# A linear-attention and mixture kernel: factors of 18 columns, x and y worked on in PSUM, ACT copying the halves, gates made for both halves by the array, and another order of the steps

## The chip, the cores and the metric

The kernel runs on one core of one Trainium2 chip. The metric is the device time of one execution in microseconds (us); of several runs the median counts. Five engines work side by side, each through its own queue in order: TensorE (PE, with its weight loads as PEld), VectorE (DVE), ScalarE (ACT), GpSimd (POOL) and SyncE (SP), which issues all the transfers here. PE writes its results to PSUM, which this kernel divides into eight tiles of 128 partitions by 512 numbers. The other tiles lie in SBUF.

## The reference

Eight batches, eight heads, 576 positions, 64 numbers per head. First a linear attention with exponential features, then a mixture of four experts with causal attention over the joined heads, two experts per position:

```python
def phi(x):
    proj = np.einsum('bhsd,df->bhsf', x, w_phi)
    proj = proj - np.max(np.abs(proj), axis=-1, keepdims=True)
    return np.concatenate([np.exp(proj), np.exp(-proj)], axis=-1)
q_p, k_p = (phi(q), phi(k))
kv = np.einsum('bhsf,bhsd->bhfd', k_p, v)
z = np.sum(k_p, axis=2)
num = np.einsum('bhsf,bhfd->bhsd', q_p, kv)
den = np.einsum('bhsf,bhf->bhs', q_p, z)[..., None] + 1e-06
attn_out = num / den
...
logits = x @ w_gate
topk = np.argpartition(-logits, K, axis=-1)[..., :K]
sel = np.take_along_axis(logits, topk, axis=-1)
w = np.exp(sel - sel.max(-1, keepdims=True))
w /= w.sum(-1, keepdims=True) + 1e-09
for e in range(E):
    q, k, v = x @ wq[e], x @ wk[e], x @ wv[e]
    scores = np.where(causal, -1000000000.0, scale * (q @ k.transpose(0, 2, 1)))
    a = np.exp(scores - scores.max(-1, keepdims=True))
    a /= a.sum(-1, keepdims=True) + 1e-09
    out += gate[e] * (a @ v @ wo[e])   # w where e is one of the two, else 0
```

Two divisions matter for what follows. The first stage divides num by den, once for each position and head. The second multiplies a @ v by the gate over the sum of the row. In both the number to multiply by is the same for all 64 numbers of a head: a *factor* per position.

## The kernel before, in words

**The order.** The kernel is written as many small generators (streams). Each yields a `Step`: an engine, the keys that it needs, whether it takes a PSUM tile, and a condition. A planner (`Plan.loop`) holds all the streams, picks among those that could start soonest the one with the lowest position, and emits its instructions; `in_order` fixes that order on each engine. Positions come from the tables at the top (`POS1` for the first stage, `POS` for the second, `BOFF` per batch, `SLOPE`, `NPOS`, `HOT`). The planner keeps its own clocks with costs per instruction (`dve`, `act`, `copies`, `PORT` for a DVE instruction that meets POOL). None of that runs on the chip; it only sets which instruction stands behind which. Eight PSUM tiles "c" are shared by all the steps: a step of PE takes one, `plan.release` gives it back.

**First stage, per pair of heads (32 pairs).** `stream_k` projects the keys (L439, and L263 for the last 64 positions), `center` takes the largest absolute value (L486) and subtracts it (L500), ACT makes both exponentials, `key_sum` adds (L473). `stream_kv` multiplies by v (L527) and makes the sums z (L543); DVE transposes the result into `kvt` (L562), which goes through DRAM (`kvd`) and comes back as `kv`. `stream_q` projects the queries (L439), ACT copies them out as `u`, POOL reduces over the partitions (L602), DVE subtracts (L604), ACT makes both exponentials. `stream_n` makes the denominators (L629), spread over four groups of 32 partitions by halves and heads, and then the numerators (L640) for the two parts of the positions, 256 and 320 wide.

**Factors.** `fractions` turns denominators (called with 'd', 32 times) or sums of the attention (called with 'y' from `sums`, 16 times) into a tile of factors laid out as the numerators are. L650: DVE transposes 288 columns from PSUM into `wided` or `widey`, in blocks of 32; the PSUM tile is released at once. L653: the nine columns that differ are taken out, plus the small constant, into `few`. For 'd', L660 makes two reciprocals of 64 partitions and L662 two copies to the other half of the partitions. For 'y', L665 makes one reciprocal and L669 four multiplications by the gate `gc`, one for each pair of source and target halves. Then ACT or DVE spreads the 18 columns to 576 (L272 or L284, `wided<-bothd`), and L675 transposes them into `xf` or `rb`.

**x and y.** `divide` multiplies the numerators in PSUM by `xf` into `xf` itself (L681) and releases the PSUM tile; a copy rounds that to `xh`, and L267 subtracts (`sub_lo`) for the rest `xl`. `evac_y` does the same with `rb` (L954), `yh` and `yl`. The next pair's `xf` may be written when both parts of x are done.

**Second stage, per batch.** `proj_t` projects queries and keys of two experts at a time (L263, weights `qk`), `proj_v` values and gate logits (`vg`), `scores` makes the scores (L768), `mask` masks on POOL (L870), `maxima` takes the maxima on DVE (L883) and over the partitions on POOL (L887), DVE subtracts (L891), ACT makes the exponentials, `sums` sums them on PE (L914), `attend` multiplies by the values (L942), `project_out` makes the output (L263, `wo`). `gates` makes the gates on DVE (L820 to L838) and spreads them with small matmuls against the identity (L849) into 20 columns, which are copied to `gc`.

Of the kernel before, what the change touches and what calls it, by code (L numbers as in the profile page):

```python
# [63 lines left out]
PORT = 500.0  # L64
OTHER = 2.37
# [172 lines left out]
def tile_linear_attn_moe(ctx, tc, qt, kt, v, wts, out):  # L238
# [104 lines left out]
    spreads = {a: [(sb(f"wide{a}{i}", [128, S]), sb(f"few{a}{i}", [128, 9]), sb(f"both{a}{i}", [128, 9, 2])) for i in range(NX)] for a in "dy"}  # L343
# [267 lines left out]
    def stream_n():  # L611


        for p in range(NPAIRS):
# [8 lines left out]
            pk, ps = yield Step('PE', Pk + [kvk], 'c', ready, tiling=(128, 32)), rank(p) + NPOS[0]
            for c in range(2):
                for half in range(2):
                    for h in range(2):
# [2 lines left out]
                        nc.tensor.matmul(ps[g:g + 32, 0:S // 2].rearrange("p (a i) -> p a i", i=32), kvi[:, 2 * h + c, 64:96],  # L629
                                         P_[h][c].rearrange("p (a b i) -> p b a i", b=2, i=32)[:, half], start=c == 0, stop=c == 1, skip_group_check=True)  # L630
            plan.spawn(fractions('d', p, ps, pk, 1e-6, xf, ['xf'], has('x', p - 1) if p else None, ('rb', p)), rank(p) + POS1['evd'])
            for s0, s1 in PARTS:
                pk, ps = yield Step('PE', Pk + [kvk], 'c', has('rb', p), tiling=(128, 32)), rank(p) + NPOS[1]
                n = s1 - s0
                for c in range(2):
                    for h in range(2):
                        for k in range(2):
                            g = 64 * k + 32 * h
# [1 line left out]
                            nc.tensor.matmul(ps[g:g + 32, 0:n], kvi[:, 2 * k + h, 32 * c:32 * c + 32], P_[h][c][:, s0:s1], start=c == 0, stop=c == 1,  # L640
                                             skip_group_check=True)
                plan.spawn(divide(p, s0, s1, pk, ps), rank(p) + POS1['div'])
            done.add(('num', p))

    def fractions(a, n, ps, pk, eps, out, wk, free, flag, gate=None):
# [4 lines left out]
        dve(S // 2, [key], [pk], 1.13).transpose(X[:, 0:S // 2], ps[:, 0:S // 2])  # L650
# [2 lines left out]
        dve(9, [bk], [key]).tensor_scalar(out=C, in0=X[:, 0:S // 2:32], scalar1=eps, scalar2=None, op0=ALU.add)  # L653
        halves = [(0, 0), (1, 1), (0, 1), (1, 0)]
        if gate is None:
            for src, dst in halves:
                r, w = slice(64 * src, 64 * src + 64), slice(64 * dst, 64 * dst + 64)
                yield Step('DVE', [bk], hot=True)
                if src == dst:
                    dve(9, [bk], [], 6.0).reciprocal(both[w, :, src], C[r])  # L660
                else:
                    dve(9, [bk], []).tensor_copy(both[w, :, src], both[r, :, src])  # L662
        else:
            yield Step('DVE', [bk], hot=True)
            dve(9, [bk], [], 6.0).reciprocal(C, C)  # L665
            for src, dst in halves:
                r, w = slice(64 * src, 64 * src + 64), slice(64 * dst, 64 * dst + 64)
                yield Step('DVE', [bk, 'gc'], pred=has('gate', n // 2), hot=True)
                dve(9, [bk], ['gc']).tensor_tensor(out=both[w, :, src], in0=C[r], in1=gate[r], op=ALU.mult)  # L669
            done.add(('gated', n))  # L670
# [4 lines left out]
        dve(S, wk, [key], 1.13).transpose(out, X)  # L675
        done.update((('wide', a, n), flag))

    def divide(p, s0, s1, pk, ps):
# [2 lines left out]
        dve(n, [('x', s0)], [pk, 'xf']).tensor_tensor(out=xf[:, s0:s1], in0=ps[:, 0:n], in1=xf[:, s0:s1], op=ALU.mult)  # L681
# [1 line left out]
        st = Step(copies_sb(n), [('x', s0)], pred=has('px', (p - PXB) // NP) if p >= PXB else None, port=True)
        yield st
        copy(st.eng, n, xT[i][0][:, s0:s1], xf[:, s0:s1], [f'xh{i}'], [('x', s0)], 0.52)
        yield Step('DVE', [f'xh{i}'])
        sub_lo(n, xT[i][1][:, s0:s1], xf[:, s0:s1], xT[i][0][:, s0:s1], f'xl{i}', [('x', s0), f'xh{i}'])
# [128 lines left out]
    def gates(b):  # L816
# [26 lines left out]
        for g in range(2):
            for a in range(2):
                for half in range(2):
                    for e in range(2):
                        r, c = 64 * half + 32 * e, 64 * a + 32 * half
                        plan.run('PE', 16, [kc], [G], tiling=(128, 32))
                        nc.tensor.matmul(o[r:r + 32, g, :, a], ident[:, c:c + 32], gw[:, 5 * (2 * g + e):5 * (2 * g + e) + 5], start=True, stop=True, skip_group_check=True)  # L849
        st = Step(copies(20), [kc], pred=lambda: not b or (('gated', 2 * b - 1) in done and ('gated', 2 * b - 2) in done), hot=True)  # L850
# [22 lines left out]
    def maxima(n):  # L873
# [29 lines left out]
    def sums(n):  # L903
# [45 lines left out]
    def evac_y(b, g, s0, s1, pk, ps):  # L949
        hi, lo = (t[:, s0:s1] for t in ys[g])  # L950
        m, i = s1 - s0, (2 * b + g) % RB
        rb = yf = rbs[i][:, s0:s1]
# [3 lines left out]
        st = Step(copies_sb(m), [('yf', i, s0)], hot=True, port=True)
        yield st
        copy(st.eng, m, hi, yf, [('yh', g, s0)], [('yf', i, s0)], 0.52)
        yield Step('DVE', [('yh', g, s0)], hot=True)
        sub_lo(m, lo, yf, hi, ('yl', g, s0), [('yf', i, s0), ('yh', g, s0)])  # L960
# [99 lines left out]
```

## Time and profile before

| | us |
|---|---|
| median of 3 runs | 689.44 |
| lowest and highest | 684.30, 689.53 |
| the profiled execution | 685.02 |
| its span, first to last instruction | 683.2 |
| ACT busy within the span | 407.9 |
| POOL busy within the span | 248.9 |

The profile is of one execution. A group's busy time is the sum of its instructions' durations. Matmuls are pipelined and the ends of their records are modelled, so a busy PE is not PE at its densest. What ended the idle time of an engine is inferred from semaphores. `ps_c` stands for any of the eight PSUM tiles, and buffer numbers are left out of the names.

### The profile page before, as it was taken

What the parts mean: (1) busy time and instruction counts of PE and PEld (TensorE: products, weight loads), DVE (VectorE), ACT (ScalarE), POOL (GpSimd) and SP (SyncE); (2) the same over time, 40 slices, a digit from 0 to 9 for tenths busy, and PEclk for the clock granted to TensorE, in tenths of its full rate; (3) what the DMA queues carried; (4) which work ended last, traced back from release to release, by engine and by line L of the source; (5) the groups of instructions that cost most, each with busy time, mean ns of one, the idle gap of its engine ahead of it and who ended that gap; (6) DMA issues with size and microseconds to landing.
All of it is one profiled execution on the core that took longest, in us unless ns stands there. A gap on an engine that the chain in (4) does not pass through costs nothing. (4 is left out here: it accounts for less than half of the span.)

```text
span 683.2 us, 20283 instructions
## 1 busy us (share of the span) xinstructions
PE 638.9 (94%) x8364; PEld 484.4 (71%) x8364; DVE 629.7 (92%) x1385; ACT 407.9 (60%) x803; POOL 248.9 (36%) x167
## 2 busy tenths in 40 slices
PE   9999998969999999979989999899999898999997
PEld 7655777547976787647776676676768666788896
DVE  6899999979999999999979999999998999899884
ACT  4876666736764685465665656765477554465462
POOL 5425235722156205720446322442524532052330
PEclk9999999979999999999999999999999999999999
DMA  6643440212223221333303234203341030101002
GB/s 188 184 132 94 109 135 21 75 45 61 63 63 106 66 79 51 100 106 106 109 2 98 74 97 124 80 28 107 98 112 49 21 113 12 48 14 70 2 35 106
DMA packets 43691, 54.34 MB, mean 80 GB/s; under 512 B 20432, under 2 KB 26576, under 8 KB 43600
## 3 DMA queue, kind: packets, MB, share of 16 engines
q1 hardware_dynamic: 43600, 53.05, 26.6%
q8 instruction: 66, 1.08, 0.7%
q14 instruction: 25, 0.20, 0.1%
HBM read 38.08 MB, written 14.94 MB: 78 GB/s over the span
## 5 line engine op out<-in xcount | busy, mean ns | idle before, releaser
L602 POOL PARTITION_ALL_REDUCE mx<-u x64 | 141.7, 2267 | 246.1 <-ACT u L272 213.9
L263 PE MATMUL ps_c<-xh,qk 128*128 128x320 f32 (+1 forms) x512 | 109.6, 304 | 2.8 <-ACT s L272 2.3
L274 ACT ACTIVATE ek<-ek 128x1152 f32<-128x1152 f32 x64 | 74.6, 1166 | 28.3 <-DVE ek L500 24.7
L870 POOL TENSOR_SCALAR_AFFINE_SELECT s<-s 128x256 f32<-128x256 f32 (+1 forms) x80 | 49.4, 639 | 115.2 <-ACT s L272 97.6
L263 PEld LDWEIGHTS ps_c<-xh,qk 128*128 128x128 f32 x512 | 85.4, 194 | 5.4 <-ACT s L272 2.6
L527 PE MATMUL ps_c<-ek,v_in 128*32 128x256 f32 x1280 | 77.3, 387 | 2.7 <-DVE xf L681 2.3
L263 PE MATMUL ps_c<-xl,qk 128*128 128x256 f32 (+1 forms) x256 | 76.9, 300 | 0.0
L887 POOL PARTITION_ALL_REDUCE max<-top x16 | 57.5, 3592 | 48.0 <-DVE top L883 33.7
L891 DVE TENSOR_TENSOR s<-s,max 128x1152 f32<-128x1152 f32 (+4 forms) x80 | 68.6, 887 | 0.5 <-POOL max L887 0.3
L274 ACT ACTIVATE s<-s 128x1152 f32<-128x1152 f32 (+4 forms) x80 | 55.2, 749 | 9.9 <-DVE s L891 9.8
L527 PEld LDWEIGHTS ps_c<-ek,v_in 128*32 128x32 f32 x1280 | 39.6, 112 | 28.8 <-issue 2.8
L263 PE MATMUL ps_c<-vg,xh 128*128 128x260 f32 (+1 forms) x320 | 59.5, 286 | 0.6 <-DVE wided L650 0.5
L263 PE MATMUL ps_c<-yh,wo 128*128 128x256 f32 (+1 forms) x256 | 54.5, 308 | 0.4 <-ACT ot L272 0.4
L486 DVE TENSOR_REDUCE pmax<-ps_c 128x4 f32<-128x512 f32 (+1 forms) x96 | 50.8, 539 | 4.0 <-PE ps_c L439 3.6
L272 ACT COPY wided<-bothd 128x576 f32<-128x576 f32 x27 | 18.1, 672 | 60.2 <-DVE bothd L662 60.2
L274 ACT ACTIVATE mx<-u 128x576 f32<-128x576 f32 x64 | 43.7, 682 | 17.2 <-DVE u L604 17.0
L272 ACT COPY s<-ps_c 128x512 f32<-128x512 f32 (+1 forms) x98 | 43.4, 535 | 16.4 <-PE ps_c L768 16.4
L500 DVE TENSOR_TENSOR ek<-ps_c,pmax 128x512 f32<-128x512 f32 (+1 forms) x96 | 51.5, 546 | 1.1
L439 PE MATMUL ps_c<-q_in,wf 64*128 64x256 f32 (+1 forms) x256 | 47.6, 424 | 4.2 <-DVE xf L681 1.6
L604 DVE TENSOR_TENSOR u<-u,mx 128x576 f32<-128x576 f32 x64 | 50.8, 804 | 0.0
L263 PEld LDWEIGHTS ps_c<-xl,qk 128*128 128x128 f32 x256 | 49.7, 194 | 0.0
L263 PEld LDWEIGHTS ps_c<-vg,xh 128*128 128x128 f32 (+1 forms) x320 | 47.3, 178 | 1.9 <-DVE wided L650 1.0
(129 smaller groups left out, 1500.2 us busy)
## 6 DMA issues: line engine op xcount, KB each, us to landing
v_in<-in_v_dram SPq DMA_DIRECT2D x32, 320.0 KB, 3.2
q_in<-in_qt_dram SPq DMA_DIRECT2D x64, 144.0 KB, 2.9
out_dram<-ot SPq DMA_DIRECT2D x32, 288.0 KB, 2.1
kvd<-kvt SPq DMA_DIRECT2D x112, 48.0 KB, 1.7
kv<-kvd SPq DMA_DIRECT2D x28, 192.0 KB, 2.6
k_in<-in_kt_dram SPq DMA_DIRECT2D x32, 160.0 KB, 3.0
k_in<-in_kt_dram SPq DMA_DIRECT2D x32, 128.0 KB, 3.0
ot<-in_wts_dram SPq DMA_DIRECT2D x10, 144.0 KB, 4.0
```

The source lines that it names most:

```text
L263: nc.tensor.matmul(o, a, b, start=start, stop=stop, skip_group_check=True)
L272: nc.scalar.copy(o, i)
L274: nc.scalar.activation(o, i, func, **kw)
L439: nc.tensor.matmul(o, a, b, start=True, stop=True, skip_group_check=True)
L486: dve(n * 128, [mk], [pk]).tensor_reduce(out=m[:, us], in_=src, axis=AX.X, op=ALU.max, apply_absolute_value=True)
L500: dve(n * 128, [e1k], [pk, mk]).tensor_tensor(out=ek2[p % EKB][:, 1, us, :], in0=src, in1=m[:, us].unsqueeze(2).to_broadcast([128, n, 128] ...
L527: nc.tensor.matmul(o[g, 0:2], v_in[:, 4 * h + t if t < 4 else 8 + h, k:64:2], ek[:, :, u_, :].rearrange("p c (w f) -> p c w f", w=4), star ...
L602: nc.gpsimd.partition_all_reduce(M, U, 128, bass_isa.ReduceOp.absmax)
L604: dve(S, [uk], [mk], port=True).tensor_tensor(out=U, in0=U, in1=M, op=ALU.subtract)
L870: nc.gpsimd.affine_select(out=d, in_=d, pattern=[[0, 2], [1, w]], compare_op=ALU.is_ge, fill=FILL, base=0, channel_multiplier=-1)
L887: nc.gpsimd.partition_all_reduce(big.rearrange("p e s -> p (e s)"), top.rearrange("p e s -> p (e s)"), 128, bass_isa.ReduceOp.max)
L891: dve(2 * (S - 128 * j), [('d', x, j)], [('max', z)], 1.11, True).tensor_tensor(out=block(s_, j), in0=block(s_, j), in1=big[:, :, 128 * j: ...
```

## The change

In `fractions` the work on the few columns moves into the PSUM tile that held the sums, in 18 columns behind the 288. ACT copies the nine columns there, once for each pair of source and target halves (four copies of 64 partitions); DVE adds the constant and takes the reciprocal over all 18 columns, and for 'y' multiplies once by a gate of 18 columns. The spreading to 576 then reads PSUM, and the tile is released after it. In `divide` and `evac_y` the product is written back to its PSUM tile; the rounding copy and the subtraction read it there, and the tile is released after the subtraction. The next `xf` waits only until both products are made. The numerators' PE step now waits until the buffers of x are free, which the rounding copy waited for before. `gates` makes the gates for both target halves with 32 calls instead of 16, in 40 columns. The positions, offsets and some costs of the planner change, and so the order of all the steps.

```diff
-HOT = 1.08
-SLOPE = (-11.47, 0.23, -2.41, -1.03, 0.53)
-NPOS = (-7.5, 3.69)
+HOT = 1.01
+SLOPE = (-15.98, 0.13, -1.38, -1.71, -2.91)
+NPOS = (-11.27, 1.84)
...
-FLEX = (54, -196)
+FLEX = (88, -161)
...
-ZEROS = 6.18
+ZEROS = 6.56
...
-POS1 = {'k': -1.53, 'q': -0.54, 'v': -1.04, 'kv': -0.44, 'z': 0.82, 'cen': 0.72, 'evu': -9.63, 'ph0': 1.68, 'ph1': 1.0, 'div': 0.45, 'evd': -3.1, 'lk': -1.44, 'lq': -1.37}
+POS1 = {'k': -1.53, 'q': -0.54, 'v': 1.13, 'kv': -0.43, 'z': 1.42, 'cen': 0.91, 'evu': -19.19, 'ph0': 1.57, 'ph1': 0.97, 'div': -0.25, 'evd': -6.77, 'lk': -1.79, 'lq': -1.14}
...
-POS = {'p0': 6.38, 'p1': -5.79, 'v0': 8.51, 'gate': 4.42, 's0': -2.57, 's1': 3.11, 'm0': 2.23, 'm1': 5.69, 't0': 6.61, 't1': 8.85, 'out': 15.11}
+POS = {'p0': 3.03, 'p1': -17.32, 'v0': 9.63, 'gate': 4.18, 's0': 4.99, 's1': -3.16, 'm0': 2.98, 'm1': 8.03, 't0': 7.27, 't1': 8.56, 'out': 15.47}
...
-PORT = 500.0
-OTHER = 2.37
+PORT = 350.0
+OTHER = 2.74
...
-    gc = sb("gc", [128, 2, NJ, 2])
+    gc = sb("gc", [128, 2, NJ, 2, 2])
...
-                pk, ps = yield Step('PE', Pk + [kvk], 'c', has('rb', p), tiling=(128, 32)), rank(p) + NPOS[1]
+                pk, ps = yield Step('PE', Pk + [kvk], 'c', lambda: ('rb', p) in done and (p < PXB or ('px', (p - PXB) // NP) in done), tiling=(128, 32)), rank(p) + NPOS[1]
...
     def fractions(a, n, ps, pk, eps, out, wk, free, flag, gate=None):
         i = n % NX
-        X, C, both = spreads[a][i]
-        key, bk = f'wide{a}{i}', f'both{a}{i}'
+        X, key = wides[a][i], f'wide{a}{i}'
+        both = ps[:, S // 2:S // 2 + 18]
+        b3 = both.rearrange("p (c d) -> p c d", d=2)
         yield Step('DVE', [pk], pred=has('wide', a, n - NX) if n >= NX else None, hot=True)
-        dve(S // 2, [key], [pk], 1.13).transpose(X[:, 0:S // 2], ps[:, 0:S // 2])
+        dve(S // 2, [key], [pk], 1.15).transpose(X[:, 0:S // 2], ps[:, 0:S // 2])
+        yield Step('ACT', [key], hot=True)
+        for src in range(2):
+            for dst in range(2):
+                r, w = slice(64 * src, 64 * src + 64), slice(64 * dst, 64 * dst + 64)
+                act(9, b3[w, :, src], X[r, 0:S // 2:32], [pk], [key])
+        yield Step('DVE', [pk], hot=True)
+        dve(18, [pk], []).tensor_scalar(out=both, in0=both, scalar1=eps, scalar2=None, op0=ALU.add)
+        dve(18, [pk], [], 5.0).reciprocal(both, both)
+        if gate is not None:
+            yield Step('DVE', [pk, 'gc'], pred=has('gate', n // 2), hot=True)
+            dve(18, [pk], ['gc']).tensor_tensor(out=both, in0=both, in1=gate, op=ALU.mult)
+            done.add(('gated', n))
+        st = Step(copies(S), [pk], hot=True)
+        yield st
+        copy(st.eng, S, X.rearrange("p (t i) -> p t i", i=32), both.unsqueeze(2).to_broadcast([128, 18, 32]), [key], [pk])
         plan.release('c', (pk, ps))
-        yield Step('DVE', [key], hot=True)
-        dve(9, [bk], [key]).tensor_scalar(out=C, in0=X[:, 0:S // 2:32], scalar1=eps, scalar2=None, op0=ALU.add)
...
     def divide(p, s0, s1, pk, ps):
         i, n = p % PXB, s1 - s0
+        x = ps[:, 0:n]
         yield Step('DVE', [pk, 'xf'], hot=True)
-        dve(n, [('x', s0)], [pk, 'xf']).tensor_tensor(out=xf[:, s0:s1], in0=ps[:, 0:n], in1=xf[:, s0:s1], op=ALU.mult)
+        dve(n, [pk], ['xf']).tensor_tensor(out=x, in0=x, in1=xf[:, s0:s1], op=ALU.mult)
+        done.add(('xd', p, s0))
+        st = Step(copies(n), [pk], hot=True)
+        yield st
+        copy(st.eng, n, xT[i][0][:, s0:s1], x, [f'xh{i}'], [pk])
+        yield Step('DVE', [f'xh{i}'], hot=True)
+        sub_lo(n, xT[i][1][:, s0:s1], x, xT[i][0][:, s0:s1], f'xl{i}', [pk, f'xh{i}'])
         plan.release('c', (pk, ps))
...
-        o = ps[:, 0:20].rearrange("p (g j a) -> p g j a", g=2, a=2)
+        o = ps[:, 0:40].rearrange("p (g j a d) -> p g j a d", g=2, a=2, d=2)
+        for g, a, half, k, e in ((g, a, half, k, e) for g in range(2) for a in range(2) for half in range(2) for k in range(2) for e in range(2)):
+                        r, c = 64 * k + 32 * e, 64 * a + 32 * half
...
     def evac_y(b, g, s0, s1, pk, ps):
...
-        rb = yf = rbs[i][:, s0:s1]
+        yf = ps[:, 0:m]
         yield Step('DVE', [pk, ('rb', i)], hot=True)
-        dve(m, [('yf', i, s0)], [pk, ('rb', i)]).tensor_tensor(out=yf, in0=ps[:, 0:m], in1=rb, op=ALU.mult)
+        dve(m, [pk], [('rb', i)]).tensor_tensor(out=yf, in0=yf, in1=rbs[i][:, s0:s1], op=ALU.mult)
+        st = Step(copies(m), [pk], hot=True)
+        yield st
+        copy(st.eng, m, hi, yf, [('yh', g, s0)], [pk])
+        yield Step('DVE', [('yh', g, s0)], hot=True)
+        sub_lo(m, lo, yf, hi, ('yl', g, s0), [pk, ('yh', g, s0)])
         plan.release('c', (pk, ps))
...
```

More of the change, by code (lines that the diff above doesn't have):

```diff
@@ L342, in tile_linear_attn_moe @@
     mx = [[sb(f"mx{i}{h}", [128, S]) for h in range(2)] for i in range(UB)]
-    spreads = {a: [(sb(f"wide{a}{i}", [128, S]), sb(f"few{a}{i}", [128, 9]), sb(f"both{a}{i}", [128, 9, 2])) for i in range(NX)] for a in "dy"}
+    wides = {a: [sb(f"wide{a}{i}", [128, S]) for i in range(NX)] for a in "dy"}
     xT = [[sb(f"x{p}{i}", [128, S], F32R) for p in "hl"] for i in range(PXB)]
@@ L630, in stream_n @@
                                          P_[h][c].rearrange("p (a b i) -> p b a i", b=2, i=32)[:, half], start=c == 0, stop=c == 1, skip_group_check=True)
-            plan.spawn(fractions('d', p, ps, pk, 1e-6, xf, ['xf'], has('x', p - 1) if p else None, ('rb', p)), rank(p) + POS1['evd'])
+            plan.spawn(fractions('d', p, ps, pk, 1e-6, xf, ['xf'], (lambda: all(('xd', p - 1, s0) in done for s0, s1 in PARTS)) if p else None, ('rb', p)), rank(p) + POS1['evd'])
             for s0, s1 in PARTS:
-                pk, ps = yield Step('PE', Pk + [kvk], 'c', has('rb', p), tiling=(128, 32)), rank(p) + NPOS[1]
+                pk, ps = yield Step('PE', Pk + [kvk], 'c', lambda: ('rb', p) in done and (p < PXB or ('px', (p - PXB) // NP) in done), tiling=(128, 32)), rank(p) + NPOS[1]
                 n = s1 - s0
@@ L653, in fractions @@
[L653 to L670, printed above, removed]
@@ L671, in fractions @@
-        st = Step((('ACT', 95 + 0.83 * S), ('DVE', 65 + 1.04 * S)), [bk], hot=True)
-        yield st
-        copy(st.eng, S, X.rearrange("p (t i) -> p t i", i=32), both.rearrange("p a b -> p (a b)").unsqueeze(2).to_broadcast([128, 18, 32]), [key], [bk])
+        dve(S // 2, [key], [pk], 1.15).transpose(X[:, 0:S // 2], ps[:, 0:S // 2])
[4 more added lines that the diff above has]
+                act(9, b3[w, :, src], X[r, 0:S // 2:32], [pk], [key])
@@ L674, in fractions @@
+        copy(st.eng, S, X.rearrange("p (t i) -> p t i", i=32), both.unsqueeze(2).to_broadcast([128, 18, 32]), [key], [pk])
+        plan.release('c', (pk, ps))
         yield Step('DVE', [key], pred=free, hot=True)
-        dve(S, wk, [key], 1.13).transpose(out, X)
+        dve(S, wk, [key], 1.1).transpose(out, X)
         done.update((('wide', a, n), flag))
@@ L679, in divide @@
         i, n = p % PXB, s1 - s0
+        x = ps[:, 0:n]
         yield Step('DVE', [pk, 'xf'], hot=True)
-        dve(n, [('x', s0)], [pk, 'xf']).tensor_tensor(out=xf[:, s0:s1], in0=ps[:, 0:n], in1=xf[:, s0:s1], op=ALU.mult)
-        plan.release('c', (pk, ps))
[L683 to L687, printed above, removed]
+        dve(n, [pk], ['xf']).tensor_tensor(out=x, in0=x, in1=xf[:, s0:s1], op=ALU.mult)
[5 more added lines that the diff above has]
+        sub_lo(n, xT[i][1][:, s0:s1], x, xT[i][0][:, s0:s1], f'xl{i}', [pk, f'xh{i}'])
+        plan.release('c', (pk, ps))
         done.add(('x', p, s0))
@@ L819, in gates @@
         yield Step('DVE', ['lg'], pred=lambda: all(('v', b, j) in done for j in range(NJ)) and (not b or ('gate', b - 1) in done))
-        dve(80, [G], ['lg']).tensor_tensor(out=ge, in0=lg.unsqueeze(3).to_broadcast(sh4),
+        dve(80, [G], ['lg'], port=True).tensor_tensor(out=ge, in0=lg.unsqueeze(3).to_broadcast(sh4),
                                            in1=lg.unsqueeze(2).to_broadcast(sh4), op=ALU.is_ge)
@@ L833, in gates @@
         yield Step('DVE', [G])
-        dve(20, [G], []).scalar_tensor_tensor(out=w, in0=lost, scalar=1.5, in1=ex, op0=ALU.is_lt, op1=ALU.mult)
+        dve(20, [G], [], port=True).scalar_tensor_tensor(out=w, in0=lost, scalar=1.5, in1=ex, op0=ALU.is_lt, op1=ALU.mult)
         dve(20, [G], []).tensor_reduce(out=gs[:, 1], in_=w, axis=AX.X, op=ALU.add)
-        dve(5, [G], []).tensor_scalar(out=gs[:, 1], in0=gs[:, 1], scalar1=1e-9, scalar2=None, op0=ALU.add)
+        dve(5, [G], [], port=True).tensor_scalar(out=gs[:, 1], in0=gs[:, 1], scalar1=1e-9, scalar2=None, op0=ALU.add)
         dve(5, [G], [], 8.0).reciprocal(gs[:, 1], gs[:, 1])
@@ L841, in gates @@
         kc, ps = yield Step('PE', [G], 'c', tiling=(128, 32))
-        o = ps[:, 0:20].rearrange("p (g j a) -> p g j a", g=2, a=2)
[L843 to L850, printed above, removed]
+        o = ps[:, 0:40].rearrange("p (g j a d) -> p g j a d", g=2, a=2, d=2)
+        for g, a, half, k, e in ((g, a, half, k, e) for g in range(2) for a in range(2) for half in range(2) for k in range(2) for e in range(2)):
+                        r, c = 64 * k + 32 * e, 64 * a + 32 * half
+                        plan.run('PE', 10, [kc], [G], tiling=(128, 32))
+                        nc.tensor.matmul(o[r:r + 32, g, :, a, half], ident[:, c:c + 32], gw[:, 5 * (2 * g + e):5 * (2 * g + e) + 5], start=True, stop=True, skip_group_check=True)
+        st = Step(copies(40), [kc], pred=lambda: not b or (('gated', 2 * b - 1) in done and ('gated', 2 * b - 2) in done), hot=True)
         yield st
-        copy(st.eng, 20, gc.rearrange("p g j a -> p (g j a)"), ps[:, 0:20], ['gc'], [kc])
+        copy(st.eng, 40, gc.rearrange("p g j a d -> p (g j a d)"), ps[:, 0:40], ['gc'], [kc])
         plan.release('c', (kc, ps))
@@ L867, in mask @@
         yield Step('POOL', skeys(x, j))
-        plan.run('POOL', 230 + 1.05 * 2 * w, [('m', x, j)], skeys(x, j))
+        plan.run('POOL', 260 + 1.3 * 2 * w, [('m', x, j)], skeys(x, j))
         d = ss[x][:, :, KEYS[j]:KEYS[j] + w]
@@ L885, in maxima @@
         yield Step('POOL', [('top', i)], pred=has('sub', n - MB) if n >= MB else None)
-        plan.run('POOL', 3600, [('max', z)], [('top', i)])
+        plan.run('POOL', 3650, [('max', z)], [('top', i)])
         nc.gpsimd.partition_all_reduce(big.rearrange("p e s -> p (e s)"), top.rearrange("p e s -> p (e s)"), 128, bass_isa.ReduceOp.max)
@@ L914, in sums @@
                     nc.tensor.matmul(ps[r:r + 32, c0:S // 2].rearrange("p (a i) -> p a i", i=32), ones, src[:, e, half], start=j == 0, stop=j == NJ - 1, skip_group_check=True)
-        yield from fractions('y', n, ps, pk, 1e-9, rbs[y], [('rb', y)], has('ys', n - RB) if n >= RB else None, ('rb2', n), gc[:, g].rearrange("p j a -> p (j a)")[:, 0:9])
+        yield from fractions('y', n, ps, pk, 1e-9, rbs[y], [('rb', y)], has('ys', n - RB) if n >= RB else None, ('rb2', n), gc[:, g].rearrange("p j a d -> p (j a d)")[:, 0:18])
     def stream_t():
@@ L951, in evac_y @@
         m, i = s1 - s0, (2 * b + g) % RB
-        rb = yf = rbs[i][:, s0:s1]
+        yf = ps[:, 0:m]
         yield Step('DVE', [pk, ('rb', i)], hot=True)
-        dve(m, [('yf', i, s0)], [pk, ('rb', i)]).tensor_tensor(out=yf, in0=ps[:, 0:m], in1=rb, op=ALU.mult)
-        plan.release('c', (pk, ps))
[L956 to L960, printed above, removed]
+        dve(m, [pk], [('rb', i)]).tensor_tensor(out=yf, in0=yf, in1=rbs[i][:, s0:s1], op=ALU.mult)
[4 more added lines that the diff above has]
+        sub_lo(m, lo, yf, hi, ('yl', g, s0), [pk, ('yh', g, s0)])
+        plan.release('c', (pk, ps))
         done.add(('y', b, g, s0))
```

4 lines of the change are left out of this document (2 added, 2 removed).

## The prediction

> **What bounds the kernel now.** I read the page's busy shares first, then the busy time by stage, then the chain that ended last, then the groups of instructions, and last the timeline around the longest stalls. The page and the table by stage (columns: stretch, length, busy of PE, PE's weight loads, DVE, ACT, POOL, granted clock, DMA share, GB/s):
>
> ```profile
> span 683.2 us, 20283 instructions
> ...
> PE 638.9 (94%) x8364; PEld 484.4 (71%) x8364; DVE 629.7 (92%) x1385; ACT 407.9 (60%) x803; POOL 248.9 (36%) x167
> ...
> PE 18%; DVE 16%; ACT 3%; issue 1%; DVEq 0%
> ```
> ```profile
> 34.00:600.00 566.00, 527.66 (x6925) 392.74 (x6922) 537.76 (x1166) 342.15 (x666) 206.68 (x129) 0.98 0.27 78
> ```
>
> Two engines are nearly full, so the mean doesn't decide. From 34 to 600 us DVE is busy 537.8 of 566 us (95%) and PE 527.7; PE is idle 38.3 us there and the granted clock is 0.98, about 11 us lost. The chain that ended last is shared between PE and DVE. How much PE really needs comes from that chain, in the stretches where PE follows itself without a wait (columns: start, length, line and count):
>
> ```profile
> 541.62 2.06 PE ps_c L439 x24
> ...
> 574.33 2.70 PE ps_c L942 x56
> 577.03 1.94 PE ps_c L640 x32
> ...
> 580.07 0.42 PE ps_c L263 x2
> 580.48 2.30 PE ps_c L527 x40
> 582.78 0.97 PE ps_c L629 x16
> ...
> 592.43 0.55 PE ps_c L543 x16
> ...
> 600.36 6.56 PE ps_c L263 x48
> ...
> 608.20 2.85 PE ps_c L768 x34
> ...
> 616.76 1.50 PE ps_c L914 x40
> ```
>
> A pair of heads has one each of the L439, L640, L527, L629, L543 blocks and the L263 x2: 8.24 us, 263.7 for 32 pairs. A batch has 204 other L263 matmuls (96 for q and k, 60 for v and gates, 48 for the output), 72 of L768, 112 of L942 and 80 of L914: 204/48 x 6.56 + 72/34 x 2.85 + 2 x 2.70 + 2 x 1.50 = 42.3 us, 338.5 for 8. With 3.5 us for the gates (row below) PE's dense work is 605.7 us. The gap to the span is 77.5 us: that is all that a relieved DVE can give back.
>
> Why DVE is late, in the groups (columns: busy us, mean ns of one; then idle before them):
>
> ```profile
> L662 DVE COPY bothd<-bothd 64x9 f32<-64x9 f32 x64 | 28.6, 447 | 1.8
> ...
> L669 DVE TENSOR_TENSOR bothy<-fewy,gc 64x9 f32<-64x9 f32 x64 | 22.2, 347 | 1.3
> ...
> L267 DVE TENSOR_TENSOR xl<-xf,xh 128x320 fp32r<-128x320 f32 x32 | 19.2, 601 | 0.1
> ...
> L267 DVE TENSOR_TENSOR xl<-xf,xh 128x256 fp32r<-128x256 f32 x32 | 18.8, 588 | 0.1
> ...
> L660 DVE RECIPROCAL bothd<-fewd 64x9 f32<-64x9 f32 x64 | 13.1, 204 | 0.9
> ...
> L653 DVE TENSOR_SCALAR fewd<-wided 128x9 f32<-128x9 f32 x32 | 9.1, 285 | 0.1
> ...
> L267 DVE TENSOR_TENSOR kkl<-ps_c,kkh 128x320 fp32r<-128x320 f32 x16 | 7.7, 479 | 1.3 <-ACT kkh L272 1.3
> ...
> L653 DVE TENSOR_SCALAR fewy<-widey 128x9 f32<-128x9 f32 x16 | 6.7, 420 | 0.2
> ...
> L267 DVE TENSOR_TENSOR kkl<-ps_c,kkh 128x256 fp32r<-128x256 f32 x16 | 6.6, 413 | 0.4 <-ACT kkh L272 0.4
> ...
> L267 DVE TENSOR_TENSOR yl<-rb,yh 128x256 fp32r<-128x256 f32 x16 | 6.6, 413 | 1.0 <-ACT yh L272 0.9
> ...
> L746 DVE COPY lg<-ps_c 128x4 f32<-128x4 f32 x32 | 3.9, 148 | 0.7 <-ACT vs L272 0.7
> ...
> L665 DVE RECIPROCAL fewy<-fewy 128x9 f32<-128x9 f32 x16 | 3.3, 207 | 0.2
> ...
> L837 DVE RECIPROCAL gs<-gs 128x5 f32<-128x5 f32 x8 | 1.5, 189 | 0.3
> ```
>
> A copy of 9 columns in SBUF costs 447 ns, a copy of 4 out of PSUM 148. The same subtraction of 256 columns costs 588 ns from xf and xh in SBUF, and 413 from PSUM. The timeline shows what lies between (columns: start, length, engine, line):
>
> ```profile
> 133.21 3.58 POOL L887 PARTITION_ALL_REDUCE max<-top  x1 [1.34 <-DVE top L883]
> 133.33 2.27 DVE L267 TENSOR_TENSOR xl<-xf,xh 128x256 fp32r<-128x256 f32 x1
> ...
> 138.61 2.36 PE L527 MATMUL ps_c<-ek,v_in 128*32 128x256 f32 x20 [2.32 <-DVE xf L681]
> ```
>
> Beside a running POOL reduction a subtraction of 413 ns took 2.27 us. PE then stood 2.32 us, until a division freed a bank, and its next 20 matmuls took 2.36 us where 40 take 2.30 above: the halved clock is paid behind the idle time.
>
> **The change, part by part.** *Factors.* The six small groups go: 9.1 + 13.1 + 28.6 + 6.7 + 3.3 + 22.2 = 83.0 us of DVE. In their place stand 48 additions, 48 reciprocals and 16 multiplications of 18 PSUM columns. An addition: 148 for 4 columns, and 14 more at (479 - 413)/64 = 1.03 ns, is 162. A reciprocal: 189 for 5 and 207 for 9, 4.5 a column, so 247 for 18. A multiplication like the addition. Sum 48 x 0.409 + 16 x 0.162 = 22.2 us. No row has DVE writing to PSUM. The input's place made no difference (kkl 413 from PSUM, yl 413 from SBUF), so I take the output's place at nothing too. The ends for these 112 and the 96 multiplications that now end in PSUM: 41 ns less each (189 - 148, the spread of small instructions), -9 us, to a whole small instruction more each (148), +31 us.
>
> [...]
>
> *x and y up to their rounding.* The subtraction of x reads PSUM: 32 x (601 - 479) + 32 x (588 - 413) ns = 9.5 us saved. That of y is already undisturbed and stays as it is.
>
> Net, DVE sheds 83.0 + 9.5 - 22.2 = 70 us. Some 48 of it are stalls beside POOL: the four 9-column groups that copy, add and multiply are 66.6 us for 176 instructions, against 28 at 160 ns, and the 9.5. Part of that may come back on the instructions that still read two SBUF tiles. The ends are none and all; yl, which reads two SBUF tiles and pays nothing, is the nearest, so I let a quarter (12) return. DVE sheds 58 us, 54 of it between 34 and 600 (45 of 48 factors): 538 becomes 484, and DVE no longer bounds that stage.
>
> *ACT.* It gets 192 copies of 9 columns:
>
> ```profile
> L272 ACT COPY gc<-ps_c 128x20 f32<-128x20 f32 x8 | 1.4, 174 | 9.9 <-PE ps_c L849 9.9
> ```
> ```profile
> L272 ACT COPY wided<-bothd 128x576 f32<-128x576 f32 x27 | 18.1, 672 | 60.2 <-DVE bothd L662 60.2
> ```
> ```profile
> DVE ql L725 <- ACT qh L274: 4.5, 9, 1.0
> ```
>
> At 174 ns they add 33 us, 408 to 441: hidden, since ACT idles a third of the span and stood 60.2 us waiting for the very factors. Their price is the new wait: DVE's addition follows ACT, with everything queued on DVE behind it, and its transpose follows ACT's broadcast as before. A like pair (ql after qh, 32 times) cost DVE 4.5 us, 0.14 each: 48 x 0.14 = 7 us, carried in full; ends 0 and 48 x 1.0.
>
> *Gates.* PE makes twice as many small matmuls, 3.5 us more (row below); the copy of 40 columns in place of 20 is nothing beside ACT's idle time. PE's dense work becomes 609.2.
>
> *Order and waits.* SP's queue, the DMAs and POOL's instructions stay as they are in number. The numerators of a pair now wait in PE's queue for a free x buffer, which the copy behind them waited for before: the same event, one step earlier. The other order has no row; I give it nothing and 10 us either way.
>
> *The sum.* What PE waits for (columns: total us, times, longest):
>
> ```profile
> PE ps_c L543 <- DVE zs L473: 10.2, 10, 2.8
> PE ps_c L629 <- DMA kv<-kvd: 5.7, 3, 3.9
> PE ps_c L849 <- DVE col L838: 5.6, 4, 2.5
> ```
>
> These three, the DMA included (it is issued behind DVE's transpose of kvt), are 21.5 of the 38.3 us idle, 56%. I let 56% of the 77.5 us gap go, 43.5: span 609.2 + 77.5 - 43.5 + 7 = 650.2. The profiled execution took 685.02 us, 1.8 over its span: 652. The median of the three runs shown is 689.44, 4.4 higher, with one run of 684.3; I say 654, between the two.
>
> **The rivals.** *The stalls come back* whole on the remaining SBUF instructions. Then DVE sheds 22 us, not 58, and 16.5 of the 43.5 is won: span 677, time 679. For it: POOL still runs its 249 us. Against: yl. [...]
>
> *Banks run short: slower.*
>
> ```profile
> 274.89 0.48 DVE L650 STREAM_TRANSPOSE widey<-ps_c 128x288 f32<-128x288 f32 x1
> ...
> 282.51 0.67 ACT L272 COPY widey<-bothy 128x576 f32<-128x576 f32 x1
> ```
> ```profile
> L849 PE MATMUL ps_c<-col,ident 128*32 128x5 f32 x256 | 3.5, 176 | 5.6 <-DVE col L838 5.6
> ```
>
> A factor's bank was free after 0.48 us; now it is held until ACT's broadcast has ended, here 8.3 us. 48 x 7.8 = 374 bank-us, and some 1.5 us more for each of 96 tiles of x and y: 518 of 8 x 683, three quarters of one of eight banks. PE waited 2.32 us for a bank once above. If each of the 48 factors costs PE one wait, it decides from (683.2 - 650.2)/48 = 0.7 us on; at 1 us the span is 698, the time 700. Against it: seven banks stay, and a chain with fewer DVE steps holds its bank for less than 8 us.
>
> *PE runs almost dense.* Where the whole visible idle time and the clock's 11 us go, the gap falls to 28 and no new wait counts: span 637, time 639, and 632 with 7 us from the order.
>
> **How the numbers follow.** The forecast's own ends: 43.5 us of span for 58 us of DVE is 0.75 each, so the unknown output in PSUM makes -7 to +23, the new wait -7 to +41. Most of that lies within 640 to 670: 0.60; almost dense, 0.12; stalls back, 670 to 685, 0.14; banks short, 0.14. A measurement tells about 1% from no change. Faster: 0.60 + 0.12 + half of the stalls' 0.14 = 0.79; same 0.07 + 0.02 of the banks' = 0.09; slower 0.12. The range 632 to 682 leaves out about 0.05 below and 0.15 above.
>
> **What would show it.** Right: DVE busy near 572; the 9-column rows gone from DVE, 18-column rows at 160 and 250 ns; xl at 479 and 413; PE's wait for zs well under 10.2; PE the busiest in every stage. Wrong: PE or its weight loads waiting on DVE's factor or subtraction steps (banks); DVE waiting on ACT's small copies by more than 0.14 each; L604, L473 and L891 longer by what the small ones lost (stalls back); DMA or ACT as the new releaser of PE.

## The result, and the profile after

| | before | changed |
|---|---|---|
| median, us | 688.99 (684.30 to 689.53, 4 runs) | 636.11 (635.93 to 638.73, 4 runs) |
| profiled execution, us | 685.02 | 635.96 |
| mean granted clock in it | 0.983 | 1.0 |

The ratio is 0.9255, 95% interval 0.9208 to 0.9303: 7.5% faster. The forecast was 654, range 632 to 682.

The page of the changed kernel, and its busy time by stage over the same stretch as before (columns as there):

```profile
span 634.2 us, 20868 instructions
...
PE 620.2 (98%) x8614; PEld 479.8 (76%) x8614; DVE 581.9 (92%) x1269; ACT 427.3 (67%) x967; POOL 244.9 (39%) x167
...
PE 73%; DVE 20%; issue 3%; ACT 3%; DMA 0%; SPq 0%; DVEq 0%; ACTq 0%
```
```profile
34.00:600.00 566.00, 558.44 (x7790) 431.81 (x7787) 531.93 (x1146) 387.27 (x881) 219.34 (x149) 1.00 0.28 81
```

PE now stands idle 634.2 - 620.2 = 14.0 us of the span, where it was 44.3 before, and it is 73% of the chain that ended last. (This chain can be followed over 99% of the span, the one before over 38% only, so their shares can't be set side by side.) DVE is busy 581.9 us, 47.8 less. The mean granted clock of that execution is 1.0. In the same 566 us PE runs 7790 matmuls, 90% of its 8614, instead of 6925, 83% of 8364.

The groups that replace those of before, and two that grew (columns: busy us, mean ns of one; then idle before them):

```profile
L604 DVE TENSOR_TENSOR u<-u,mx 128x576 f32<-128x576 f32 x64 | 58.1, 924 | 1.4 <-POOL mx L602 1.4
...
L473 DVE TENSOR_TENSOR zs<-zs,ek 128x512 f32<-128x512 f32 x56 | 44.2, 789 | 0.4
...
L272 ACT COPY ps_c<-wided 64x9 f32<-64x9 f32 x128 | 22.0, 172 | 12.7 <-DVE wided L651 9.2
...
L676 DVE TENSOR_TENSOR ps_c<-ps_c,xf 128x320 f32<-128x320 f32 x32 | 15.6, 487 | 0.0
...
L267 DVE TENSOR_TENSOR xl<-ps_c,xh 128x320 fp32r<-128x320 f32 x32 | 14.9, 467 | 0.0
...
L659 DVE RECIPROCAL ps_c<-ps_c 128x18 f32<-128x18 f32 x48 | 13.4, 278 | 1.6
...
L267 DVE TENSOR_TENSOR xl<-ps_c,xh 128x256 fp32r<-128x256 f32 x32 | 13.2, 411 | 0.5 <-ACT xh L272 0.3
...
L658 DVE TENSOR_SCALAR ps_c<-ps_c 128x18 f32<-128x18 f32 x48 | 8.2, 171 | 0.8 <-ACT ps_c L272 0.7
...
L842 PE MATMUL ps_c<-col,ident 128*32 128x5 f32 x512 | 5.7, 175 | 1.7 <-DVE col L834 1.7
...
L662 DVE TENSOR_TENSOR ps_c<-ps_c,gc 128x18 f32<-128x18 f32 x16 | 2.7, 169 | 0.1
```

The additions and multiplications on the few columns now cost about 170 ns each, where the groups that copied, added and multiplied before cost 285 to 447. The first two groups above, as they were in the kernel before:

```profile
L604 DVE TENSOR_TENSOR u<-u,mx 128x576 f32<-128x576 f32 x64 | 50.8, 804 | 0.0
...
L473 DVE TENSOR_TENSOR zs<-zs,ek 128x512 f32<-128x512 f32 x56 | 40.0, 714 | 0.5
```

Both read two SBUF tiles, and each grew by 11 to 15% in the mean with no work added.

Of PE's waits, the three that were longest before have all but gone (columns: total us, times, longest):

```profile
PE ps_c L842 <- DVE col L834: 1.7, 1, 1.7
PE ps_c L543 <- DVE zs L473: 1.1, 1, 1.1
```

The wait for the sums zs was 10.2 us, that for the gates 5.6, and that for the transfer of kv, 5.7 us before, has no row.

### The profile page after: what moved, and what is told of

Read it like the earlier page. It is cut to its first block, busy times and chain, and to the rows that moved or that the text cites. A ratio compares the mean times of both kernels' runs of the same rounds, so it can differ in the third digit from the quotient of the medians.

```text
span 634.2 us, 20868 instructions
## 1 busy us (share of the span) xinstructions
PE 620.2 (98%) x8614; PEld 479.8 (76%) x8614; DVE 581.9 (92%) x1269; ACT 427.3 (67%) x967; POOL 244.9 (39%) x167
## 4 chain that ended last, share of the span: by engine, by line
PE 73%; DVE 20%; issue 3%; ACT 3%; DMA 0%; SPq 0%; DVEq 0%; ACTq 0%
PE ps_c L263 31%; PE ps_c L527 9%; PE ps_c L439 8%; PE ps_c L640 6%; PE ps_c L935 6%; PE ps_c L764 5%; PE ps_c L629 3%; PE ps_c L907 3%; DVE zs L473 2%; DVE top L876 2%; PE ps_c L543 2%; DVE pmax L486 2%; DVE ek L500 2%; DVE u L604 2%; DVE ps_c L676 1%
## 5 line engine op out<-in xcount | busy, mean ns | idle before, releaser
L263 PE MATMUL ps_c<-xh,qk 128*128 128x320 f32 (+1 forms) x512 | 105.5, 296 | 0.0
L863 POOL TENSOR_SCALAR_AFFINE_SELECT s<-s 128x256 f32<-128x256 f32 (+1 forms) x80 | 44.7, 583 | 140.7 <-ACT s L272 67.3
L263 PEld LDWEIGHTS ps_c<-xh,qk 128*128 128x128 f32 x512 | 82.5, 187 | 1.7 <-DVE u L284 0.5
L527 PE MATMUL ps_c<-ek,v_in 128*32 128x256 f32 x1280 | 75.5, 381 | 1.6 <-ACT ek L274 0.8
L263 PE MATMUL ps_c<-xl,qk 128*128 128x256 f32 (+1 forms) x256 | 75.2, 294 | 0.0
L884 DVE TENSOR_TENSOR s<-s,max 128x1152 f32<-128x1152 f32 (+4 forms) x80 | 70.4, 905 | 0.4 <-POOL max L880 0.4
L274 ACT ACTIVATE s<-s 128x1152 f32<-128x1152 f32 (+4 forms) x80 | 56.2, 738 | 11.0 <-DVE s L884 10.5
L527 PEld LDWEIGHTS ps_c<-ek,v_in 128*32 128x32 f32 x1280 | 39.5, 110 | 27.6 <-ACT ek L274 1.0
L604 DVE TENSOR_TENSOR u<-u,mx 128x576 f32<-128x576 f32 x64 | 58.1, 924 | 1.4 <-POOL mx L602 1.4
L935 PE MATMUL ps_c<-s,vs 128*32 128x320 f32 (+4 forms) x896 | 46.3, 357 | 0.0
L263 PE MATMUL ps_c<-vg,xl 128*128 128x260 f32 (+1 forms) x160 | 45.0, 281 | 0.0
L439 PE MATMUL ps_c<-q_in,wf 64*128 64x256 f32 (+1 forms) x256 | 44.0, 426 | 0.9 <-ACT u L272 0.5
```

Source lines behind the costliest of these rows:

```text
L263: nc.tensor.matmul(o, a, b, start=start, stop=stop, skip_group_check=True)
L274: nc.scalar.activation(o, i, func, **kw)
L439: nc.tensor.matmul(o, a, b, start=True, stop=True, skip_group_check=True)
L527: nc.tensor.matmul(o[g, 0:2], v_in[:, 4 * h + t if t < 4 else 8 + h, k:64:2], ek[:, :, u_, :].rearrange("p c (w f) -> p c w f", w=4), star ...
L604: dve(S, [uk], [mk], port=True).tensor_tensor(out=U, in0=U, in1=M, op=ALU.subtract)
L863: nc.gpsimd.affine_select(out=d, in_=d, pattern=[[0, 2], [1, w]], compare_op=ALU.is_ge, fill=FILL, base=0, channel_multiplier=-1)
```

## The experiments

In the first four kernels, and in `eps_act`, the instructions of each engine stand in the same order as in the changed kernel, so the order is not what differs. The others are planned anew. The changed kernel was timed in one session and the experiments in three others; the kernel before, run beside each, had medians from 686.7 to 689.0 us. Differences of 2 us between sessions therefore tell nothing.

**1. The small factors in SBUF** (`small_sbuf`), in a tile of 18 columns for each kind. The PSUM tile is then free for PE after the first transpose already, a second difference, in this kernel's favour.

```diff
-        both = ps[:, S // 2:S // 2 + 18]
+        both = few[a]
```

> The changed kernel with the 18 columns of the factors kept in an SBUF tile instead of PSUM; each engine's instructions stand in the same order. Theory 'stalls' (the gain comes from DVE no longer meeting POOL): the 48 additions go from 171 ns to 300 to 400 and the 16 multiplications from about 170 to 350, the reciprocals stay near 278 or below; DVE's busy time rises by 8 to 14 us from 581.9, the time by 5 to 10 us, to 641 to 646. Rival 'fewer instructions' (the gain comes from 144 instructions less): all of them stay under 200 ns, the time within 3 us of 636.

Measured: 644.54 us, ratio to before 0.9383 (0.9356 to 0.9410); DVE busy 590.9 us. The groups of this kernel:

```profile
L658 DVE TENSOR_SCALAR fewd<-fewd 128x18 f32<-128x18 f32 x32 | 10.4, 326 | 0.6 <-ACT fewd L272 0.6
...
L658 DVE TENSOR_SCALAR fewy<-fewy 128x18 f32<-128x18 f32 x16 | 7.5, 472 | 0.1
...
L662 DVE TENSOR_TENSOR fewy<-fewy,gc 128x18 f32<-128x18 f32 x16 | 5.5, 344 | 0.1
...
L659 DVE RECIPROCAL fewy<-fewy 128x18 f32<-128x18 f32 x16 | 4.3, 266 | 0.6
```

The same additions cost 326 and 472 ns in SBUF against 171 in PSUM, the multiplications 344 against 169, the reciprocals no more (266 against 278). Laid beside POOL's instructions in the timeline of this trace, the 29 additions that overlap none took 0.13 to 0.18 us, and the 19 that overlap one took 0.70 us in the mean and up to 1.94. In the changed kernel 21 of the 48 overlap one, and they took 0.17 us like the others. So it is beside POOL that these additions are dear, and only in SBUF. DVE's busy time rises by 9.0 us and the time by 8.4, as the theory of the stalls had it.

**2. The products x and y in SBUF** (`xy_sbuf`): xf and rb take them as before, and a spare tile `xr` of 320 columns the second part of x.

```diff
-        x = ps[:, 0:n]
+        x = xr if s0 else xf[:, s0:s1]
...
-        yf = ps[:, 0:m]
+        yf = rbs[i][:, s0:s1]
```

> The changed kernel with the products x and y put into SBUF (xf, a spare tile of 320 columns, and rb) and rounded and subtracted from there; same order on each engine. Theory 'stalls': the subtractions of x go from 467 and 411 ns to about 600 and 590, DVE's busy time rises by 8 to 12 us, the time by 5 to 10, to 641 to 646. Rival 'fewer instructions': no price, within 3 us of 636.

Measured: 641.33 us, 0.9335 (0.9304 to 0.9365).

```profile
L267 DVE TENSOR_TENSOR xl<-xr,xh 128x320 fp32r<-128x320 f32 x32 | 17.9, 560 | 0.0
...
L267 DVE TENSOR_TENSOR xl<-xf,xh 128x256 fp32r<-128x256 f32 x32 | 16.5, 517 | 0.7 <-ACT xh L272 0.4
```

The subtractions grow by 93 and 106 ns, 6 us in all, somewhat less than expected; DVE's busy time rises by only 3.2 us, under the expected 8 to 12, and the time by 5.2.

**3. Both** (`both_sbuf`).

> Both of the above at once, same order: nothing of the change's work in PSUM, but its few instructions, ACT's copies and its order stay. [...] Rival 'fewer instructions': 636 to 640.

Measured: 647.12 us, 0.9428 (0.9395 to 0.9461); DVE busy 593.3 us, 11.4 more where the theory of the stalls had 18 to 25, clock 0.997. The time rises by 11.0 us and ends between the 650 to 658 of that theory and the 636 to 640 of its rival. Taking the work that stays on DVE out of SBUF is thus worth 11 of the 53 us in this order. The larger part lies elsewhere.

**4. The halves copied by DVE** (`halves_dve`).

```diff
-                act(9, b3[w, :, src], X[r, 0:S // 2:32], [pk], [key])
+                plan.run('ACT', 95 + 0.83 * 9, [pk], [key]); nc.vector.tensor_copy(b3[w, :, src], X[r, 0:S // 2:32])
```

> The changed kernel with the 192 copies of nine columns made by DVE instead of ACT, at the same places of the order, into the same PSUM columns. Theory 'DVE's time still counts': 192 x 0.15 to 0.17 us, no stalls since one side is PSUM, DVE busy 581.9 + 29 to 33, time 655 to 666. Rival 'PE bounds now': the time stays below 645. If the copies do meet POOL (300 ns or more each) the time goes over 670.

Measured: 668.97 us, 0.9736 (0.9708 to 0.9763). The page of this kernel, and its new group:

```profile
span 667.4 us, 20820 instructions
...
PE 636.6 (95%) x8614; PEld 487.4 (73%) x8614; DVE 609.5 (91%) x1461; ACT 396.0 (59%) x775; POOL 245.8 (37%) x167
...
PE 45%; DVE 43%; ACT 5%; issue 4%; DMA 2%; POOL 1%; DVEq 0%; SPq 0%; ACTq 0%; POOLq 0%
```
```profile
L656 DVE COPY ps_c<-wided 64x9 f32<-64x9 f32 x128 | 21.8, 170 | 3.3
```

At 170 ns each the copies do not stall. Yet the time is 3 us above even the end that the theory of DVE's time had, with DVE's busy time 27.6 us up and the time 32.9. DVE and PE share the chain again, the listed waits of PE on DVE add up to 19.5 us instead of 7.2, and the clock fell to 0.987.

**5. The same, with an order made for it** (`halves_dve_plan`): the planner places the copies on DVE and counts them there.

```diff
-        yield Step('ACT', [key], hot=True)
+        yield Step('DVE', [key], hot=True)
...
-                act(9, b3[w, :, src], X[r, 0:S // 2:32], [pk], [key])
+                dve(9, [pk], [key]).tensor_copy(b3[w, :, src], X[r, 0:S // 2:32])
```

> The 192 small copies on DVE as before in halves_dve, but the planner knows it and makes the order for it. Theory 'the 31 us of DVE count in any order': 655 to 668. Rival 'the 33 us were the price of an order that did not fit': 645 or less.

Measured: 673.92 us, 0.9806 (0.9778 to 0.9833), 6 us over the expected end. So the price of experiment 4 is not that of an order which didn't fit.

**6. Less still for DVE** (`eps_act`): ACT's copies add the small constant, and DVE's 48 additions go.

```diff
-                act(9, b3[w, :, src], X[r, 0:S // 2:32], [pk], [key])
+                plan.run('ACT', 95 + 0.83 * 9, [pk], [key]); nc.scalar.activation(b3[w, :, src], X[r, 0:S // 2:32], AF.Copy, bias=eps)
...
-        dve(18, [pk], []).tensor_scalar(out=both, in0=both, scalar1=eps, scalar2=None, op0=ALU.add)
+        plan.run('DVE', 65 + 1.04 * 18, [pk], [])
```

> The changed kernel with the small constant added by ACT's four copies (as their bias) and DVE's 48 additions left out; the other instructions in the same order. Theory 'DVE's time still counts, about 1 us for 1 us': 48 x 0.171 = 8.2 us of DVE less, the time 5 to 9 us down, 627 to 631. Rival 'PE bounds now': 634 to 637. If the bias makes ACT's copies much dearer than 172 ns and DVE waits for them, no gain or a loss.

Measured: 635.72 us, 0.9251 (0.9226 to 0.9276), no difference from the changed kernel.

```profile
PE 619.8 (98%) x8614; PEld 480.1 (76%) x8614; DVE 577.5 (91%) x1221; ACT 429.3 (68%) x967; POOL 243.0 (38%) x167
```

DVE is 4.4 us less busy (8.2 were expected), PE as busy as in the changed kernel. The result lies in the rival's range: these 4.4 us of DVE gain nothing. With experiments 1 to 4 that puts the changed kernel at the knee: in this order, above 582 us of DVE a microsecond of it costs about one (8.4 for 9.0; 5.2 for 3.2; 11.0 for 11.4; 32.9 for 27.6, with the clock), and 4.4 us below it gain nothing.

**7. Order and instructions apart** (`order_only`, `old_order`). Only the constants at the top of the diff are exchanged: all of them in the kernel before, and the reverse in the changed one. One of the lines:

```diff
-POS = {'p0': 6.38, 'p1': -5.79, ...
+POS = {'p0': 3.03, 'p1': -17.32, ...
```

> The kernel before with the constants of the changed one (positions, offsets, planner's costs): another order and nothing else. Theory 'the instructions count': within 1.5% of 689, 679 to 699. Rival 'the order does it': 665 or less.

> The changed kernel with the constants of the one before. Theory 'the instructions count': 636 to 650, the order worth at most 14 us. Rival 'the order does it': 660 or more.

Measured: the new constants alone 695.84 us, 1.0114 (1.0080 to 1.0147), a little slower; the new instructions under the old constants 662.93 us, 0.9622 (0.9595 to 0.9650). From the page of the latter:

```profile
span 661.4 us, 20865 instructions
...
PE 630.2 (95%) x8620; PEld 478.7 (72%) x8620; DVE 584.9 (88%) x1263; ACT 430.3 (65%) x973; POOL 244.7 (37%) x167
```

DVE is about as little busy as in the changed kernel (584.9 against 581.9), but PE is idle 31.2 us instead of 14.0. Three of the waits behind that, which have no row in the changed kernel (columns: total us, times, longest):

```profile
PE ps_c L629 <- DMA kv<-kvd: 4.3, 3, 3.7
...
PE ps_c L935 <- ACT ot L272: 2.7, 2, 2.0
PE ps_c L263 <- ACT u L272: 2.1, 5, 0.5
```

Added up by what ended them, PE's listed waits (40.1 of its 44.3 us of idle time, 26.9 of 31.2, and 10.0 of 14.0) are, in us:

| | DVE | ACT | DMA |
|---|---|---|---|
| before | 28.2 | 5.6 | 6.3 |
| new instructions, old constants | 8.0 | 13.1 | 5.8 |
| changed | 7.2 | 2.6 | 0.2 |

The new instructions take away the waits on DVE, and under the old constants those on ACT grow; the new constants take away the waits on ACT and on the DMAs. The first kernel fits "the instructions count", the second "the order does it"; neither theory holds for both. The instructions alone are worth 25 us (687.92, the kernel before beside these runs, to 662.93), and the order, worth nothing or less by itself, another 27 once they are there (25 by the ratios). Which of the constants does it was not tried and stays open.

**8. One part alone, under the new constants** (`factors_only`, `xy_only`). The first is the changed kernel with `divide`, `evac_y` and their waits as before, the second the kernel before with these in their new form and the new constants. One line of the first:

```diff
-        dve(n, [pk], ['xf']).tensor_tensor(out=x, in0=x, in1=xf[:, s0:s1], op=ALU.mult)
+        dve(n, [('x', s0)], [pk, 'xf']).tensor_tensor(out=xf[:, s0:s1], in0=ps[:, 0:n], in1=xf[:, s0:s1], op=ALU.mult)
```

> The changed kernel with the x and y steps of the one before (products in SBUF, banks released at once, the old waits), new order. Theory 'stalls': the subtractions of x cost about 600 again, 9 us of DVE; time 641 to 655. If the factors carry all of the gain, 636 to 640; if x and y carry most, over 660.

> The kernel before with the new x and y steps, its old factors and gates, and the new order. Theory 'stalls': the old factors' 83 us of DVE stay, so 670 to 685. If x and y carry most of the gain, under 660.

Measured: factors 656.99 us, 0.9529 (0.9490 to 0.9568), just over the expected 655; x and y 687.58 us, 0.9996 (0.9976 to 1.0015), just over the expected 685. In the first the subtractions of x cost 697 and 510 ns, 10.5 us more than in the changed kernel. Under the same constants, then: neither 695.8, x and y 687.6, factors 657.0, both 636.1. The factors are worth 39 us alone, x and y 8, both 60. Each of these is planned anew, so an unknown part of the differences is order, and the 8 us for x and y are no more than the shift of experiment 9 makes.

**9. How much an order costs that nothing speaks for** (`shift1`).

```diff
-BOFF = (0.74, 1.43, -0.41, 0.08, -0.01, 1.61, 2.01, 3.54)
+BOFF = (0.74, 1.53, -0.41, 0.08, -0.01, 1.61, 2.01, 3.54)
```

> The changed kernel with the offset of the second batch moved by 0.1 (1.43 to 1.53): the same instructions in another order from about there on. It measures how much an order costs that nothing speaks for or against: 634 to 646 if single steps matter little; over 650 if the time hangs on the exact order as much as on the instructions.

Measured: 643.62 us, 0.9370 (0.9339 to 0.9400). That is within the end for "single steps matter little", yet an offset moved by 0.1 costs 7.5 us. Differences of that size between kernels that were planned anew tell nothing of their instructions.

**10. One PSUM tile fewer** (`psum7`).

```diff
-PSUM_TILES = (("c", 8, 512),)
+PSUM_TILES = (("c", 7, 512),)
```

> The changed kernel with seven PSUM tiles instead of eight, planned anew. Theory 'banks are not short': 636 to 645, PE's waits little longer. Rival 'banks are short since the change holds them longer': 655 or more.

Measured: 652.16 us, 0.9480 (0.9450 to 0.9510): 16 us, between the two expectations and twice what a mere shift costs. DVE's busy time is 580.4 us, so the loss isn't DVE's. The eighth tile may be worth some 8 us beyond the other order, but one shift is too few to say so.

## Why the prediction was right, and where it was not

**Right.** The direction, and the reason for about half of the gain: DVE held PE up. The waits of PE on DVE fell from 28.2 to 8.0 us by the new instructions alone (experiment 7), that for zs from 10.2 to 1.1 in the changed kernel. The prices came out near their rows. The additions took 171 ns (162 forecast), the multiplications 169 (162), the reciprocals 278 (247), the subtractions of x 467 and 411 (479 and 413), ACT's copies 172 (174). The 18-column instructions add up to 48 x 0.449 + 2.7 = 24.3 us against 22.2.

**PE's dense work, 609.2 us, was counted too low.** The span stands 25.0 us over it, 14.0 of them idle. The count has 16 matmuls of L543 for each pair, but four pairs have 40 (about 3.6 us more by the timeline), and it leaves out 12 of L554 (2.2 us) and 90 on the tile `warm` (7.4 us): some 13 us, against the 11 that are not idle. So almost nothing is left to gain beyond the idle time, and that lies mostly before 200 us and after 600. From 200 to 550 us PE stands idle 1.2 us in all; one of these stretches (columns as in the table by stage):

```profile
350.00:400.00 50.00, 50.00 (x668) 39.20 (x667) 47.90 (x106) 38.10 (x85) 21.37 (x10) 1.00 0.36 105
```

This fits experiment 6, where less work for DVE gained nothing. "538 becomes 484, and DVE no longer bounds that stage" did not come: DVE stays 94% busy from 34 to 600 us, since PE gets through more of its work there, and by experiments 1 to 4 more work for DVE costs time at once.

**DVE's relief: 47.8 us, where the forecast had 58.** The quarter of the stalls that I let return (12 us) was in the sum, and L604 and the running L473 grew by about that, 7.3 and 4.2 us. But in `old_order`, with the same new instructions, they took 812 and 722 ns, 0.9 us more than before in all. So that growth comes with the new constants, and not, as I argued, with the instructions. What the sum did not have is that the planner gives DVE more of the copies (L284): they add up to 56.5 us, and to 54.4 in `old_order`, where DVE's relief is 44.8 us; before they were 39.1. The evidence for the quarter was also weak: in the trace before, 31 of the 32 subtractions yl overlap no POOL instruction, so they could show no price. In `factors_only` those of 256 columns cost 533 ns.

**"I let 56% of the 77.5 us gap go", and 7 us come back: 36.5 us net were forecast, 52.5 went.** The gap to 609.2 is 25.0 where the sum had 41. The clock's share did not shrink in proportion, it vanished: 1 - 0.983 of a span of 683 us is 11.6 us (behind the wait of 2.32 us the granted clock was 0.50 from 138.6 to 141.0 us), and the clock is 1.0 after. The idle time of PE lost 30.3 us. The other 10.6 us lie in PE's busy time, and their cause stays open. The new wait, carried at 7 us, came to 0.7 of DVE's time (the row of L658).

**"The other order has no row; I give it nothing and 10 us either way": this step failed.** By experiment 7 the new order is worth 27 us to the new instructions, and costs 8 to the old ones. The instructions under the old order gave 25 us, less than the 33 that the sum had for them. For each microsecond of DVE's relief that is 0.56, against 33 for 58, 0.57, in the sum; where a single shift moves 7.5 us, so close an agreement may be chance. The forecast of 654 lies between the two results because it over-priced the instructions by 8 us and under-priced the order by 27; that the time stayed within the range is in part luck. That an order's worth depends on the instructions it orders was not in the sum at all. The waits show where: ACT's added work was taken as hidden, but under the old constants PE's waits on ACT grew from 5.6 to 13.1 us, and the new constants brought them to 2.6. DMA or ACT as the new releaser of PE was named as a sign of being wrong; it is there in `old_order` and gone in the changed kernel.

**The stalls were sized rightly, but putting work into PSUM is the smaller part of the cure.** The prediction laid 48 of the 83 + 9.5 us on POOL. In the trace before, the 33 of the 64 copies L662 that overlap no POOL instruction took 0.17 us, and the 31 that overlap one took 0.74 us in the mean; over all of the groups that the prediction named, the overlapping ones cost about 50 us more than the others. But many of these instructions leave DVE altogether. For those that stay, the place in PSUM is worth 11 us in the final order (experiment 3); that ACT and not DVE makes the 192 copies, which do not stall on DVE either (170 ns each), is worth 33 (experiment 4). While DVE held PE up here, what counted was how long DVE was busy, stalled or not.

**The rivals.** That the stalls come back whole is refuted: on L604 and L473 they came to 0.9 us under the old constants and to 11.5 under the new ones. That banks run short did not show with eight: no wait of PE or its weight loads on the factors, the products or the subtractions was over 0.5 us. With seven tiles the time is 16 us longer, of which half may be the other order. "Almost dense" (637 us of span) is nearest to what came, with 634.2: it was given 0.12, too little.

## What to carry to other kernels

Where two engines are both nearly full (94 and 92% here), work out the dense time of the one from the stretches where it follows itself, with every matmul counted, and go by the distance to it, not by the other's busy share. What a microsecond of the other engine is worth is no constant: in the final order more work for DVE cost about one for one (8.4 us for 9.0 in experiment 1) and less gained nothing (experiment 6), while under the old constants 44.8 us of relief gave 25. Small instructions from SBUF to SBUF that met POOL's were cheaper here in the PSUM tile that their data was in already (additions at 171 ns against 326 and 472), and copies moved from DVE to ACT, which was idle a third of the span, brought more (33 us against 8). A change of the instructions and a change of their order are not to be added up: try the one under the other's order before giving either a price.

## What the runs showed of the hardware that was not expected

- A DVE multiplication that writes back to PSUM took 487 and 424 ns (L676), against 479 and 409 into SBUF before (L681): 8 and 15 ns more. The subtractions of x, which now read PSUM, took 467 and 411 ns, against 601 and 588 from SBUF before.
- ACT's copy of nine columns took 172 ns into PSUM and 205 into SBUF (`small_sbuf`, below). A constant added in that copy costs 12 ns (184, `eps_act`).
- The one run of the changed kernel that had a clock of 0.996 took 638.73 us, 2.5 to 2.8 more than those at 1.0.

The rows: the multiplications of x, after and before, then ACT's copies in `small_sbuf` and `eps_act`.

```profile
L676 DVE TENSOR_TENSOR ps_c<-ps_c,xf 128x320 f32<-128x320 f32 x32 | 15.6, 487 | 0.0
...
L676 DVE TENSOR_TENSOR ps_c<-ps_c,xf 128x256 f32<-128x256 f32 x32 | 13.6, 424 | 3.6 <-PE ps_c L640 3.4
```
```profile
L681 DVE TENSOR_TENSOR xf<-ps_c,xf 128x320 f32<-128x320 f32 x32 | 15.3, 479 | 1.1 <-PE ps_c L640 1.1
...
L681 DVE TENSOR_TENSOR xf<-ps_c,xf 128x256 f32<-128x256 f32 x32 | 13.1, 409 | 0.4 <-PE ps_c L640 0.3
```
```profile
L272 ACT COPY fewd<-wided 64x9 f32<-64x9 f32 x128 | 26.2, 205 | 10.2 <-DVE wided L651 8.8
```
```profile
L656 ACT ACTIVATE ps_c<-wided 64x9 f32<-64x9 f32 x128 | 23.5, 184 | 12.8 <-DVE wided L651 9.4
```
